# A fused routing-attention and SwiGLU kernel: a new start, later weight loads, and the norm ahead of the output products

## The chip, the cores and the metric

The kernel runs on one core of one Trainium2 chip. The metric is the device time of one execution in microseconds, lower is better. The reported time is the median of three runs. One more execution was taken by the hardware profiler, and all rows below come from that one.

## What is computed

Attention in which each query sees only the keys that were assigned to the same one of 16 centroids, then a gated feed-forward layer with an RMS norm. All inputs are float32. The shapes are q, k, v (4, 8, 768, 64), centroids (8, 16, 64), 3072 tokens of width 512 and a hidden width of 1536.

```python
q_assign = argmax(q_n @ c_n.T);  k_assign = argmax(k_n @ c_n.T)     # per head, 16 clusters
scores = where(q_assign[:, None] == k_assign[None, :], q @ k.T / 8, -1e9)
x = softmax(scores) @ v                                              # then heads side by side: (3072, 512)
xn = x / sqrt(mean(x * x) + 1e-6) * rms_g
out = (silu(xn @ w_gate) * (xn @ w_val)) @ w_out
```

## The kernel before

**Groups and units.** The 32 (batch, head) pairs form eight groups of four heads (`HG`). A group is prepared once: TensorE transposes q and k of each head (`trans`, L171, two parts of three 128x128 tiles), ScalarE copies the result out (L172), GpSimd and VectorE cast it to bfloat16 into `qext` and `kext` (L174, L175), GpSimd casts v (`vcast`, L178), and `scores_c` (L185) finds the cluster of each row: TensorE products with the centroids, four VectorE passes per half (L192, L196, L198, L203), and small DMAs that write one-hot rows under `qext` and `kext` (L206, L207). The score product then has 64 + 16 rows, so the mask comes out of the same product.

The attention itself runs in eight units u (`NU`), one for each half (384 queries) of a batch. A unit goes over eight heads h with three steps i each: `scores(u, h, i)` is two TensorE products into one of two PSUM tiles and one ScalarE exponential (L222). At i = 0, `pv` of the head before (L236) follows, and after each second head VectorE divides by the sum (L240, L242). Unit u uses groups 2b and 2b + 1 of its batch b = u // 2.

**Fill.** Between the steps, the main loop (L392 to L424) spreads a list of other work by a cost in front of each entry. In unit u these are the output products of unit u - 2 (`out_mm`, L318, nine pieces), the feed-forward of unit u - 1 (`rms`, `xtrans`, `gv`) and the preparation of group u + 2. `rms(u)` is three ScalarE squares over the last two heads (L254), a chain of eleven short VectorE operations on 128x3 numbers, and three scalings into `xn` (L279). TensorE can transpose `xn` (L288) only after that. The instruction order on every engine is the order of the code.

**Loads.** q and k have six staging buffers (`NQ`), v eight (`NV`). SP issues nearly all loads. The weights are cast in flight, on GpSimd's queue (`load_gv`, `load_o`). Before the first unit group 0 and half of group 1 are prepared; weights and the first loads of the second batch (`more`, L378) follow during it. The DMAs of SP and ScalarE share eight landing semaphores of the program, so an issue can wait for the landing of an earlier one.

Of the kernel before, what the change touches and what calls it, by code (L numbers as in the profile page):

```python
# [22 lines left out]
def kernel(  # L23
# [69 lines left out]
        load_qk(n, nc.scalar)  # L93
    for n in range(HG, NQ):
        load_qk(n)
    for n in range(HG):
        load_v(n, nc.scalar)
    gcol = const.tile([P, CC], F32)


# [2 lines left out]
    warm_ps = ps_s.tile([P, 2, 512], F32, tag="s", name="warm")  # L103
    for i in range(WARM):
        nc.tensor.matmul(warm_ps[:, i % 2], lhsT=warm[:, :P], rhs=warm, start=True, stop=True)


    ones = const.tile([P, P], F32)
# [18 lines left out]
        nc.gpsimd.memset(vbf[i][:, :, :, D:D + 1], 1.0)  # L127
    off = const.tile([P, 1], F32)
    nc.gpsimd.memset(off, -scale * ZS)


    c_sq = const.tile([P, D], F32)
    c_ss = const.tile([P, 1], F32)
    nc.vector.tensor_mul(c_sq, c_in, c_in)
    nc.vector.reduce_sum(c_ss, c_sq, axis=AX)
    c_inv = const.tile([P, 1], F32)
    nc.vector.reciprocal(c_inv, c_ss)
    nc.scalar.activation(c_inv, c_inv, ACT.Sqrt)
# [5 lines left out]
    c_ps = ps_g.tile([P, P], F32, tag="gen")
    nc.tensor.transpose(c_ps, c_n, ident_f)
    nc.vector.tensor_copy(cblk[:D, :, :NC], c_ps[:D].rearrange("d (h c) -> d h c", c=NC))
    nc.vector.tensor_copy(cblk[D:, :, NC:], c_ps[D:].rearrange("d (h c) -> d h c", c=NC))
# [13 lines left out]

    qkT = {}

    def trans(g, h, part):
        if (h, part) == (0, 0):
            qkT[g] = qk32.tile([P, HG, S], F32, tag="qkT", name="qkT")
        qk = staged[g * HG + h]
        ps = ps_g.tile([P, UQ], F32, tag="gen", name="tq")
        for i in range(HT):
            t = part * HT + i  # L170
            nc.tensor.transpose(ps[:, i * P:(i + 1) * P], qk[:, t].rearrange("p a d -> p (a d)"), ident_f)  # L171
        nc.scalar.copy(qkT[g][:, h, part * UQ:(part + 1) * UQ], ps)  # L172
        if part:
            nc.gpsimd.tensor_copy(qext[g % 4][:D, h], qkT[g][:D, h])  # L174
            nc.vector.tensor_scalar_mul(kext[g % 4][:D, h], qkT[g][D:, h], 1.0 / ZS)  # L175

    def vcast(n):
        nc.gpsimd.tensor_copy(vbf[n // HG % 4][:, n % HG, :, :D], stagedv[n])  # L178
# [3 lines left out]

    ohs = {}

    def scores_c(g, m, h0=0, h1=HG):  # L185
        ps = ps_g.tile([P, UQ], F32, tag="gen", name="sc")
        r = slice(32 * h0, 32 * h1)
        for h in range(h0, h1):
            nc.tensor.matmul(ps[32 * h:32 * h + 32], lhsT=cblk[:, g * HG % H + h],  # L189
                             rhs=qkT[g][:, h, m * UQ:(m + 1) * UQ], start=True, stop=True)  # L190
        sct = asg.tile([P, UQ], F32, tag="scT", name="scT", bufs=2)
        nc.vector.transpose(sct[r], ps[r])  # L192
        n = UQ // NC
        cl = sct[r].rearrange("p (n c) -> p n c", c=NC)
        mx = small.tile([P, n], F32, tag="mx", name="mx")
        nc.vector.tensor_reduce(mx[r], cl, axis=AX, op=ALU.max)  # L196
        ohT = asg.tile([P, UQ], BF16, tag="ohT", name="ohT", bufs=2)
        nc.vector.tensor_tensor(ohT[r].rearrange("p (n c) -> p n c", c=NC), cl,  # L198
                                mx[r].unsqueeze(2).broadcast_to([32 * (h1 - h0), n, NC]), op=ALU.is_equal)
        if m == 0:  # L200
            ohs[g, h0] = asg.tile([P, S], BF16, tag="oh", name="oh", bufs=2)
        oh = ohs[g, h0]
        nc.vector.transpose(oh[r, m * UQ:(m + 1) * UQ], ohT[r])  # L203
        if m:
            for h in range(h0, h1):
                nc.sync.dma_start(out=qext[g % 4][D:D + NC, h], in_=oh[32 * h:32 * h + NC])  # L206
                nc.sync.dma_start(out=kext[g % 4][D:D + NC, h], in_=oh[32 * h + NC:32 * h + 2 * NC])  # L207


    pT = {}  # L210
# [10 lines left out]
                             rhs=qext[g % 4][:KR, hh, hf * UQ:(hf + 1) * UQ], start=True, stop=True)  # L221
        nc.scalar.activation(pT[u, h][:, 2 * i:2 * i + 2], ps[:, :, :UQ], ACT.Exp, bias=off, scale=scale * ZS)  # L222

    xs, accs = {}, {}

    def pv(u, h):
        b = u // 2
        g, hh = b * 2 + h // HG, h % HG
        if h == 0:
            xs[u] = xp.tile([P, HT, DM], F32, tag="x", name="x", bufs=2)  # L230
        if h % 2 == 0:
            accs[u] = ps_a.tile([P, 2, HT, D + 1], F32, tag="acc", name="acc")
# [23 lines left out]
    def rms(u):  # L256
        x = xs[u]
        for t in range(HT):
            squares(u, t, True)
        ss = small.tile([P, HT], F32, tag="sm", name="sm")  # L260
        nc.vector.tensor_add(ss, sq[u][:, 0], sq[u][:, 1])
        ms = small.tile([P, HT], F32, tag="ms", name="ms")
        nc.vector.tensor_scalar(ms, ss, 1.0 / DM, 1e-6, op0=ALU.mult, op1=ALU.add)
        half = small.tile([P, HT], I32, tag="half", name="half")
        nc.vector.tensor_scalar(half, ms.bitcast(I32), 1, None, op0=ALU.logical_shift_right)
        yi = small.tile([P, HT], I32, tag="yi", name="yi")
        nc.vector.tensor_scalar(yi, half, -1.0, float(0x5F3759DF), op0=ALU.mult, op1=ALU.add)
        y = yi.bitcast(F32)
        for i in range(3):
            a = small.tile([P, HT], F32, tag="na", name="na")  # L270
            nc.vector.scalar_tensor_tensor(a, y, -0.5, y, op0=ALU.mult, op1=ALU.mult)
            a2 = small.tile([P, HT], F32, tag="nb", name="nb")
            nc.vector.tensor_mul(a2, a, ms)
            y2 = small.tile([P, HT], F32, tag="ny", name="ny")
            nc.vector.scalar_tensor_tensor(y2, a2, 1.5, y, op0=ALU.add, op1=ALU.mult)
            y = y2
        xn[u] = xp.tile([P, HT, DM], BF16, tag="xn", name="xn")
        for t in range(HT):
            nc.vector.tensor_scalar_mul(xn[u][:, t], x[:, t], y[:, t:t + 1])  # L279
# [48 lines left out]
            nc.sync.dma_start(out=rows[:, hf * HT + t], in_=o)  # L328


    def group_work(g, loads=True):
        w = []
        for h in range(HG):
            n = g * HG + h
# [1 line left out]

            def second(h=h, n=n):
                trans(g, h, 1)
                vcast(n)
                if loads:  # L340
                    load_qk(n + NQ)
                    load_v(n + NV)
            w.append((0.25, second))
# [14 lines left out]
        return w  # L358

    def ffn_work(u):  # L360
        w = [(0.0, lambda: rms(u))] + [(0.18, lambda c=c: xtrans(u, c)) for c in range(CC)]
        for f in range(FC):
            w.append((0.64, lambda f=f: gv(u, f, False)))
            w.append((0.64, lambda f=f: gv(u, f, True)))
        return w
# [2 lines left out]
        return [(0.86, lambda t=t, p=p: out_mm(u, t, p)) for t in range(HT) for p in range(3)]  # L368


    for h in range(HG):
        for part in range(2):
            trans(0, h, part)
        if NQ + h < H:
            load_qk(NQ + h)
        if h % 2:
            for m in range(2):
                scores_c(0, m, h - 1, h + 1)  # L378
    for n in range(HG, H):
        load_v(n)  # L380
    for h in range(HG):
        vcast(h)
        if h % 2:
            load_gv(h - 1)
    nc.sync.dma_start(out=gcol, in_=moe_rms_g.rearrange("(c p) -> p c", p=P), allow_slow_non_contiguous=True)
    first = group_work(1, False)
    for _, f in first[:4]:
        f()
    load_gv(1)
    load_gv(3)  # L390

    for u in range(NU):  # L392
        fill = []
        if u >= 2:
            fill += out_work(u - 2)
        prep = group_work(u + 2) if u + 2 < NG else []
        if u == 0:
            def more():
                for c in range(0, FC, 4):
                    load_o(c)  # L400
                for n in range(H, H + NV):
                    if n < H + NQ:
                        load_qk(n)
                    load_v(n)
            fill = first[4:] + [(0.0, more)] + prep
        elif u == 1:
            fill = prep[:4] + spread(ffn_work(0), prep[4:])
        else:
            fill += spread(ffn_work(u - 1), prep)
        total = sum(c for c, _ in fill)  # L410
# [47 lines left out]
```

## Time and profile before

| | |
|---|---|
| median of three runs | 449.36 us (447.55 to 450.74) |
| profiled execution | 448.44 us |
| its span in the profile | 446.7 us |
| TensorE busy, share of span | 370.0 us, 83% |
| ScalarE busy | 257.1 us, 58% |
| VectorE busy | 249.0 us, 56% |
| GpSimd busy | 57.9 us, 13% |
| mean granted TensorE clock | 0.907 |

The span is what the profile sees; 1.7 us of the execution's time lie around it. A matmul's end in the profile is modelled, so a busy TensorE may still be slow: the granted clock has to be read beside it (1.0 is 2.4 GHz, 0.5 is 1.2 GHz).

### The profile page before, as it was taken

How to read it: one execution, taken by the hardware profiler on the slowest of the kernel's cores; microseconds unless marked ns; L12 is line 12 of the kernel's file. 1: busy time of each engine (PE TensorE's matmuls, PEld its weight loads, DVE VectorE, ACT ScalarE, POOL GpSimd, SP SyncE). 2: the span in 40 equal slices, each digit the busy share in tenths (PEclk: the TensorE clock that was granted, in tenths of full speed). 3: DMA queues.
4: the chain of work that ended last, by engine and by line, in shares of the span. 5: the costliest groups of instructions: out<-in, count | busy, mean ns of one | idle time of the engine just before them, and what ended most of it. 6: DMA issues, size and time to landing. Idle time of an engine off the chain costs nothing.

```text
span 446.7 us, 7733 instructions
## 1 busy us (share of the span) xinstructions
PE 370.0 (83%) x3003; PEld 223.9 (50%) x3017; DVE 249.0 (56%) x550; ACT 257.1 (58%) x452; POOL 57.9 (13%) x84
## 2 busy tenths in 40 slices
PE   4793086699969998799969996999959995997896
PEld 1361063466536654566536653665536652663452
DVE  3764027567654784567557675478455535554441
ACT  1373088387836775377637873678536863783130
POOL 0627043111001210112002200121000000000000
PEclk8859589699988999899989999799979997999699
DMA  9598998422022422224113002000100010001001
GB/s 237 129 216 154 210 288 229 115 54 54 11 79 54 106 57 66 58 73 107 34 57 72 1 8 83 0 2 1 66 23 2 0 48 26 0 1 56 16 0 72
DMA packets 63732, 32.00 MB, mean 72 GB/s; under 512 B 52944, under 2 KB 59600, under 8 KB 63696
## 3 DMA queue, kind: packets, MB, share of 16 engines
q1 hardware_dynamic: 57248, 25.21, 20.9%
q0 software_dynamic: 2736, 4.72, 6.1%
q10 hardware_dynamic: 3712, 1.57, 1.3%
q8 instruction: 24, 0.39, 0.3%
q14 instruction: 12, 0.10, 0.1%
HBM read 28.35 MB, written 6.29 MB: 78 GB/s over the span
## 4 chain that ended last, share of the span: by engine, by line
PE 67%; DVE 13%; ACT 10%; DMA 6%; issue 3%; SPq 0%; ACTq 0%; DVEq 0%
PE o L323 14%; PE gate L299 13%; PE s L220 12%; PE val L299 12%; PE acc L236 7%; ACT pT L222 6%; PE tq L171 4%; PE sc L189 3%; DMA qk<-in_k_dram 2%; DVE xn L279 2%; DVE kext L175 2%; DMA qk<-in_q_dram 2%; PE tx L288 2%; ACT junk L254 2%; ACT qkT L172 1%
## 5 line engine op out<-in xcount | busy, mean ns | idle before, releaser
L222 ACT ACTIVATE pT<-s,off 128x768 bf16<-128x768 f32 x192 | 172.5, 902 | 87.2 <-PE s L220 86.8
L220 PE MATMUL s<-qext,kext 80*128 80x384 bf16 x384 | 99.9, 345 | 1.7 <-ACT pT L222 1.6
L299 PE MATMUL gate<-xnT,wg 128*128 128x384 bf16 x384 | 83.6, 342 | 0.8 <-DVE xnT L289 0.8
L299 PE MATMUL val<-xnT,wv 128*128 128x384 bf16 x384 | 80.2, 332 | 0.0
L309 DVE SCALAR_TENSOR_TENSOR gu<-th,gate 128x384 f32<-128x384 f32 x84 | 46.3, 551 | 52.1 <-ACT th L307 52.0
L323 PE MATMUL o<-wo,gvT 128*128 128x512 bf16 x274 | 68.2, 378 | 0.8
L174 POOL CAST qext<-qkT 64x768 bf16<-64x768 f32 x32 | 31.7, 991 | 241.5 <-ACT qkT L172 241.4
L171 PE MATMUL tq<-ident_f,qk 128*128 128x128 f32 x192 | 38.3, 326 | 21.8 <-DMA qk<-in_k_dram 17.3
L307 ACT ACTIVATE th<-gate 128x384 f32<-128x384 f32 x84 | 41.0, 488 | 26.7 <-PE gate L299 26.7
L220 PEld LDWEIGHTS <-kext 80*128 80x128 bf16 x384 | 38.0, 104 | 35.7 <-issue 12.2
L236 PEld LDWEIGHTS <-pT 128*128 128x128 bf16 x1152 | 47.9, 99 | 14.6 <-ACT pT L222 5.2
L236 PE MATMUL acc<-vbf,pT 128*128 128x65 bf16 x1152 | 51.5, 196 | 3.7 <-ACT pT L222 3.3
L314 DVE SCALAR_TENSOR_TENSOR gvT<-gu,val 128x384 bf16<-128x384 f32 x84 | 46.5, 554 | 11.8 <-PE val L299 5.1
L299 PEld LDWEIGHTS <-wg 128*128 128x128 bf16 x384 | 37.6, 102 | 25.5 <-issue 5.8
L299 PEld LDWEIGHTS <-wv 128*128 128x128 bf16 x384 | 37.2, 99 | 23.4 <-issue 1.9
L172 ACT COPY qkT<-tq 128x384 f32<-128x384 f32 x64 | 30.0, 478 | 32.1 <-issue 18.2
L175 DVE TENSOR_SCALAR kext<-qkT 64x768 bf16<-64x768 f32 x32 | 29.0, 912 | 34.3 <-ACT qkT L172 33.8
L288 PE MATMUL tx<-ident,xn 128*128 128x128 bf16 x96 | 15.4, 300 | 37.2 <-DVE xn L279 36.0
L171 PEld LDWEIGHTS tq<-ident_f,qk 128*128 128x128 f32 x192 | 28.3, 169 | 32.3 <-issue 19.1
L323 PEld LDWEIGHTS <-gvT 128*128 128x128 bf16 x288 | 26.7, 97 | 27.0
L326 DVE COPY o_sb<-o 128x512 f32<-128x512 f32 x24 | 16.6, 692 | 37.5 <-PE o L323 37.2
L288 PEld LDWEIGHTS <-xn 128*128 128x128 bf16 x96 | 9.9, 133 | 44.5 <-DVE xn L279 43.5
(56 smaller groups left out, 206.8 us busy)
## 6 DMA issues: line engine op xcount, KB each, us to landing
qk<-in_q_dram SPq DMA_DIRECT2D x32, 192.0 KB, 3.4
out_dram<-o_sb SPq DMA_DIRECT2D x24, 256.0 KB, 2.0
qk<-in_k_dram SPq DMA_DIRECT2D x28, 192.0 KB, 3.7
vs<-in_v_dram SPq DMA_DIRECT2D x28, 192.0 KB, 3.5
wg<-in_moe_w_gate_dram POOLq DMA_DIRECT2D x4, 384.0 KB, 5.8
wv<-in_moe_w_val_dram POOLq DMA_DIRECT2D x4, 384.0 KB, 7.2
wo<-in_moe_w_out_dram POOLq DMA_DIRECT2D x3, 512.0 KB, 11.6
qk<-in_k_dram ACTq DMA_DIRECT2D x4, 192.0 KB, 4.5
```

Source lines behind the costliest of these rows:

```text
L171: nc.tensor.transpose(ps[:, i * P:(i + 1) * P], qk[:, t].rearrange("p a d -> p (a d)"), ident_f)
L172: nc.scalar.copy(qkT[g][:, h, part * UQ:(part + 1) * UQ], ps)
L175: nc.vector.tensor_scalar_mul(kext[g % 4][:D, h], qkT[g][D:, h], 1.0 / ZS)
L220: nc.tensor.matmul(ps[:, j, :UQ], lhsT=kext[g % 4][:KR, hh, kc * P:(kc + 1) * P], rhs=qext[g % 4][:KR, hh, hf * UQ:(hf + 1) * UQ], start=T ...
L222: nc.scalar.activation(pT[u, h][:, 2 * i:2 * i + 2], ps[:, :, :UQ], ACT.Exp, bias=off, scale=scale * ZS)
L236: nc.tensor.matmul(acc[:, h % 2, t], lhsT=pT[u, h][:, kc, t * P:(t + 1) * P], rhs=vbf[g % 4][:, hh, kc], start=kc == 0, stop=kc == ST - 1)
L288: nc.tensor.transpose(ps[:, t * P:(t + 1) * P], xn[u][:, t, c * P:(c + 1) * P], ident)
L299: nc.tensor.matmul(ps, lhsT=w[:, c, f * P:(f + 1) * P], rhs=xnT[u][:, c], start=c == 0, stop=c == CC - 1)
L307: nc.scalar.activation(th, ps, ACT.Tanh, scale=0.5)
L309: nc.vector.scalar_tensor_tensor(gu, th, 1.0, ps, op0=ALU.add, op1=ALU.mult)
L314: nc.vector.scalar_tensor_tensor(gvT[u][:, f], gates[u], 0.5, ps, op0=ALU.mult, op1=ALU.mult)
L323: nc.tensor.matmul(outs[u], lhsT=gvT[u][:, f, t * P:(t + 1) * P], rhs=wo[:, f], start=f == 0, stop=f == FC - 1)
```

## The change

**Start.** The centroid norm is computed by a Newton iteration on VectorE in place of ScalarE's square root; ScalarE loads its exponential table at the very beginning. For group 0, ScalarE also writes `kext` from PSUM (new L194), the cluster scores take the PSUM tiles of the score product, and the one-hot DMAs are issued by ScalarE in place of SP. Four v loads are no longer on ScalarE's queue.

**Loads.** All weight loads stand behind the eight v casts of the first batch. The second batch's loads stand behind a small DMA (`hold`) that reads the reciprocal of heads 4 and 5 of unit 0.

**Order.** Group 2 is prepared in unit 1 with group 3, no longer in unit 0. `rms(u - 1)` is issued in the second step of unit u, ahead of the output products' later parts.

```diff
...
-    for n in range(HG):
-        load_v(n, nc.scalar)
+    for n in range(2):
+        load_v(n)
...
+    first_exp = const.tile([P, 1], F32)
+    nc.scalar.activation(first_exp, off, ACT.Exp)
...
-    c_inv = const.tile([P, 1], F32)
-    nc.vector.reciprocal(c_inv, c_ss)
-    nc.scalar.activation(c_inv, c_inv, ACT.Sqrt)
+    c_inv = rsqrt(c_ss, 1)
...
-        nc.scalar.copy(qkT[g][:, h, part * UQ:(part + 1) * UQ], ps)
-        if part:
-            nc.gpsimd.tensor_copy(qext[g % 4][:D, h], qkT[g][:D, h])
-            nc.vector.tensor_scalar_mul(kext[g % 4][:D, h], qkT[g][D:, h], 1.0 / ZS)
+        c = slice(part * UQ, (part + 1) * UQ)
+        nc.scalar.copy(qkT[g][:, h, c], ps)
+        if early:
+            nc.scalar.activation(kext[g % 4][:D, h, c], ps[D:], ACT.Copy, scale=1.0 / ZS)
...
-                nc.sync.dma_start(out=qext[g % 4][D:D + NC, h], in_=oh[32 * h:32 * h + NC])
-                nc.sync.dma_start(out=kext[g % 4][D:D + NC, h], in_=oh[32 * h + NC:32 * h + 2 * NC])
+                q_ = nc.scalar if early else nc.sync
+                q_.dma_start(out=qext[g % 4][D:D + NC, h], in_=oh[32 * h:32 * h + NC])
+                q_.dma_start(out=kext[g % 4][D:D + NC, h], in_=oh[32 * h + NC:32 * h + 2 * NC])
...
-        w = [(0.0, lambda: rms(u))] + [(0.18, lambda c=c: xtrans(u, c)) for c in range(CC)]
+        w = [(0.18, lambda c=c: xtrans(u, c)) for c in range(CC)]
...
+    def second_batch():
+        nc.sync.dma_start(out=hold, in_=invs[0].rearrange("p a t -> p (a t)"))
+        for n in range(H, H + NV):
+            if n < H + NQ:
+                load_qk(n)
+            load_v(n)
...
-        prep = group_work(u + 2) if u + 2 < NG else []
+        prep = group_work(u + 2) if 2 <= u < NG - 2 else []
...
-            fill = first[4:] + [(0.0, more)] + prep
+            fill = first[4:] + [(0.0, weights)]
         elif u == 1:
-            fill = prep[:4] + spread(ffn_work(0), prep[4:])
+            prep = group_work(2) + group_work(3)
+            fill = prep[:6] + spread(ffn_work(0), prep[6:])
...
-        gaps, done, n = 3 * H, 0.0, 0
+        gaps, done, n = 3 * H if u else 6, 0.0, 0
...
+                    if (u, h) == (0, H - 2):
+                        second_batch()
+                if (h, i) == (0, 1) and u:
+                    rms(u - 1)
...
     pv(NU - 1, H - 1)
+    rms(NU - 1)
     for _, f in out_work(NU - 2) + ffn_work(NU - 1) + out_work(NU - 1):
```

ScalarE's order at the start of the program, before (`qkT<-tq` copies a transposed head out, `pT<-s,off` is an exponential):

```order
L82 DMA qk<-in_k_dram 128x6x64 x4
L88 DMA vs<-in_v_dram 128x384 x4
L138 ACT_TABLE_LOAD
L138 ACTIVATE c_inv<-c_inv 128x1
L172 COPY qkT<-tq 128x384 x12
L222 ACT_TABLE_LOAD
L222 ACTIVATE pT<-s,off 128x768
```

The same engine after, from the last part of head 2 of group 0 to the first exponential (`oh` are the one-hots that VectorE makes):

```order
L192 COPY qkT<-tq 128x384
L194 ACTIVATE kext_147<-tq 64x384
L239 DMA qext_143<-oh 16x768
L240 DMA kext_147<-oh 16x768
...
L192 COPY qkT<-tq 128x384
L194 ACTIVATE kext_147<-tq 64x384
...
L239 DMA qext_143<-oh 16x768
L240 DMA kext_147<-oh 16x768
...
L192 COPY qkT<-tq 128x384 x4
L255 ACTIVATE pT<-s,off 128x768
```

The issues of the one-hots now stand between ScalarE's copies, four behind head 2 and four behind head 3.

VectorE's order at the start of unit 2, before (`inv` and `x` close a pair of heads, `o_sb` is an output row block, `sm` begins the norm, `xnT` follows the transposes of `xn`):

```order
L240 RECIPROCAL inv<-acc 128x6
L242 TENSOR_TENSOR x<-acc,inv 128x2x3x64
L326 COPY o_sb<-o 128x512 x2
L240 RECIPROCAL inv<-acc 128x6
L242 TENSOR_TENSOR x<-acc,inv 128x2x3x64
L326 COPY o_sb<-o 128x512
L261 TENSOR_TENSOR sm<-ss 128x3
...
L279 TENSOR_SCALAR xn<-x,ny 128x512 x3
L289 TENSOR_SCALAR xnT<-tx,gcol 128x384 x4
```

And after, at the same place:

```order
L274 RECIPROCAL inv<-acc 128x6
L276 TENSOR_TENSOR x<-acc,inv 128x2x3x64
L295 TENSOR_TENSOR sm<-ss 128x3
...
L301 TENSOR_SCALAR xn<-x,ny 128x512 x3
L348 COPY o_sb<-o 128x512 x2
L274 RECIPROCAL inv<-acc 128x6
L276 TENSOR_TENSOR x<-acc,inv 128x2x3x64
L348 COPY o_sb<-o 128x512
L311 TENSOR_SCALAR xnT<-tx,gcol 128x384 x4
```

The norm now stands directly behind the division of heads 6 and 7, and the three output copies behind it.

## Rows read from the trace of the kernel before

**Rows 1.** Waits: engine, line, waited for: us total, times, longest.

```profile
PE tx L288 <- DVE xn L279: 36.0, 13, 5.5
```

**Rows 2.** Stretches: busy us (x instructions) by engine, granted clock, DMA share, GB/s.

```profile
66.00:76.00 10.00, 7.42 (x89) 4.38 (x90) 6.42 (x13) 8.62 (x18) 1.75 (x3) 1.00 0.99 256
84.00:117.00 33.00, 32.74 (x308) 20.71 (x306) 20.96 (x41) 26.34 (x43) 3.20 (x4) 0.96 0.24 61
```

**Rows 3.** Timeline from the start of unit 2: start, us, instruction [idle before].

```profile
118.76 0.56 DVE L242 TENSOR_TENSOR x<-acc,inv 128x384 f32<-128x384 f32 x1
...
119.55 0.90 ACT L222 ACTIVATE pT<-s,off 128x768 bf16<-128x768 f32 x1 [1.48 <-PE s L220]
...
121.74 0.74 PE L236 MATMUL acc<-vbf,pT 128*128 128x65 bf16 x18
...
127.81 0.30 ACT L254 ACTIVATE junk<-x 128x128 bf16<-128x128 f32 x1
...
129.10 0.16 DVE L261 TENSOR_TENSOR sm<-ss 128x3 f32<-128x3 f32 x1
...
131.67 1.28 DVE L279 TENSOR_SCALAR xn<-x,ny 128x512 bf16<-128x512 f32 x3
...
132.22 1.40 PE L288 MATMUL tx<-ident,xn 128*128 128x128 bf16 x6 [3.87 <-DVE xn L279]
```

**Rows 4.** Timeline of TensorE: restarts in unit 1, unit 6 and behind unit 7.

```profile
82.17 2.07 PE L288 MATMUL tx<-ident,xn 128*128 128x128 bf16 x12 [5.51 <-DVE xn L279]
...
329.16 1.08 PE L288 MATMUL tx<-ident,xn 128*128 128x128 bf16 x3 [5.24 <-DVE xn L279]
...
415.06 1.19 PE L288 MATMUL tx<-ident,xn 128*128 128x128 bf16 x4 [3.75 <-DVE xn L279]
```

**Rows 5.** Seven stretches behind restarts (units 2 to 7, end): first, last, sum.

```profile
132.20:138.00 5.80, 5.38 (x25) 3.58 (x26) 2.51 (x7) 1.92 (x4) 0.00 (x0) 0.50 0.00 0
...
415.10:421.30 6.20, 5.98 (x26) 3.31 (x27) 2.65 (x7) 0.78 (x2) 0.00 (x0) 0.50 0.01 3
sum 40.00, PE 37.40 PEld 23.92 DVE 17.94 ACT 12.79 POOL 0.03; mean PE 5.34 PEld 3.42 DVE 2.56 ACT 1.83 POOL 0.00
```

**Rows 6.** Timeline: group 2's first transpose in unit 0, unit 1's first exponential.

```profile
55.87 0.87 PE L171 MATMUL tq<-ident_f,qk 128*128 128x128 f32 x3 [17.34 <-DMA qk<-in_k_dram]
...
74.46 0.89 ACT L222 ACTIVATE pT<-s,off 128x768 bf16<-128x768 f32 x1
```

**Rows 7.** Chain that ended last: start, us, what.

```profile
1.18 3.58 DMA qk<-in_q_dram
...
39.06 5.33 DMA qext<-oh
...
45.10 10.63 DMA qk<-in_k_dram
```

**Rows 8.** DMA queues, 48.6 to 48.7 us: packets, MB, share of 16 engines.

```profile
q0 software_dynamic: 16, 0.02, 96.2%
q1 hardware_dynamic: 11, 0.00, 21.3%
```

**Rows 9.** DMA queues over the whole span: GpSimd's queue, the weights.

```profile
q0 software_dynamic: 2736, 4.72, 6.1%
```

**Rows 10.** Timeline of the start.

```profile
11.28 0.48 ACT L172 COPY qkT<-tq 128x384 f32<-128x384 f32 x1 [1.66 <-PE tq L171]
...
14.66 0.57 DVE L192 STREAM_TRANSPOSE scT<-sc 64x384 f32<-64x384 f32 x1 [0.40 <-PE sc L189]
...
19.27 0.60 SPq L206 DMA_DIRECT2D qext<-oh  x1
...
27.19 0.90 ACT L222 ACTIVATE pT<-s,off 128x768 bf16<-128x768 f32 x1
```

**Rows 11.** Timeline of TensorE in unit 1: three transposes; eight cluster products.

```profile
97.57 0.49 PE L171 MATMUL tq<-ident_f,qk 128*128 128x128 f32 x3
...
109.86 0.85 PE L189 MATMUL sc<-qkT,cblk 128*32 128x384 f32 x8
```

More of the change, by code (lines that the diff above doesn't have):

```diff
@@ L105, with rsqrt @@
         nc.tensor.matmul(warm_ps[:, i % 2], lhsT=warm[:, :P], rhs=warm, start=True, stop=True)
+    def rsqrt(ms, n):
+        half = small.tile([P, n], I32, tag=f"half{n}", name="half")
+        nc.vector.tensor_scalar(half, ms.bitcast(I32), 1, None, op0=ALU.logical_shift_right)
+        yi = small.tile([P, n], I32, tag=f"yi{n}", name="yi")
+        nc.vector.tensor_scalar(yi, half, -1.0, float(0x5F3759DF), op0=ALU.mult, op1=ALU.add)
+        y = yi.bitcast(F32)
+        for i in range(3):
+            a = small.tile([P, n], F32, tag=f"na{n}", name="na")
+            nc.vector.scalar_tensor_tensor(a, y, -0.5, y, op0=ALU.mult, op1=ALU.mult)
+            a2 = small.tile([P, n], F32, tag=f"nb{n}", name="nb")
+            nc.vector.tensor_mul(a2, a, ms)
+            y2 = small.tile([P, n], F32, tag=f"ny{n}", name="ny")
+            nc.vector.scalar_tensor_tensor(y2, a2, 1.5, y, op0=ALU.add, op1=ALU.mult)
+            y = y2
+        return y
     ones = const.tile([P, P], F32)
@@ L143, with centroids_t @@
     nc.vector.memset(cblk, 0.0)
[L144 to L147, printed above, removed]
+    def centroids_t():
+        c_ps = ps_g.tile([P, P], F32, tag="gen", name="c_ps")
+        nc.tensor.transpose(c_ps, c_n, ident_f)
+        nc.vector.tensor_copy(cblk[:D, :, :NC], c_ps[:D].rearrange("d (h c) -> d h c", c=NC))
+        nc.vector.tensor_copy(cblk[D:, :, NC:], c_ps[D:].rearrange("d (h c) -> d h c", c=NC))
     wg = const.tile([P, CC, DF], BF16)
@@ L162, with trans @@
     qkT = {}
-    def trans(g, h, part):
+    def trans(g, h, part, early=False):
         if (h, part) == (0, 0):
@@ L171, in trans, with qcast, kcast @@
             nc.tensor.transpose(ps[:, i * P:(i + 1) * P], qk[:, t].rearrange("p a d -> p (a d)"), ident_f)
-        nc.scalar.copy(qkT[g][:, h, part * UQ:(part + 1) * UQ], ps)
-        if part:
-            nc.gpsimd.tensor_copy(qext[g % 4][:D, h], qkT[g][:D, h])
-            nc.vector.tensor_scalar_mul(kext[g % 4][:D, h], qkT[g][D:, h], 1.0 / ZS)
+        c = slice(part * UQ, (part + 1) * UQ)
+        nc.scalar.copy(qkT[g][:, h, c], ps)
+        if early:
+            nc.scalar.activation(kext[g % 4][:D, h, c], ps[D:], ACT.Copy, scale=1.0 / ZS)
+    def qcast(g, h):
+        nc.gpsimd.tensor_copy(qext[g % 4][:D, h], qkT[g][:D, h])
+    def kcast(g, h):
+        nc.vector.tensor_scalar_mul(kext[g % 4][:D, h], qkT[g][D:, h], 1.0 / ZS)
     def vcast(n):
@@ L183, with scores_c @@
     ohs = {}
-    def scores_c(g, m, h0=0, h1=HG):
-        ps = ps_g.tile([P, UQ], F32, tag="gen", name="sc")
+    scps = {}
+    def scores_c(g, m, h0=0, h1=HG, early=False):
+        if not early:
+            ps = ps_g.tile([P, UQ], F32, tag="gen", name="sc")
+        else:
+            if m == 0:
+                scps[g, h0] = ps_s.tile([P, 2, 512], F32, tag="s", name="sc")
+            ps = scps[g, h0][:, m, :UQ]
         r = slice(32 * h0, 32 * h1)
@@ L222, in scores @@
         nc.scalar.activation(pT[u, h][:, 2 * i:2 * i + 2], ps[:, :, :UQ], ACT.Exp, bias=off, scale=scale * ZS)
-    xs, accs = {}, {}
+    xs, accs, invs = {}, {}, {}
     def pv(u, h):
@@ L239, in pv @@
             inv = small.tile([P, 2, HT], F32, tag="inv", name="inv")
+            invs[u] = inv
             nc.vector.reciprocal(inv, acc[:, :, :, D])
@@ L263, in rms @@
         nc.vector.tensor_scalar(ms, ss, 1.0 / DM, 1e-6, op0=ALU.mult, op1=ALU.add)
[L264 to L276, printed above, removed]
+        y = rsqrt(ms, HT)
         xn[u] = xp.tile([P, HT, DM], BF16, tag="xn", name="xn")
@@ L328, in out_mm, with group_work @@
             nc.sync.dma_start(out=rows[:, hf * HT + t], in_=o)
-    def group_work(g, loads=True):
+    def group_work(g):
         w = []
@@ L338, in second @@
                 trans(g, h, 1)
+                qcast(g, h)
+                kcast(g, h)
                 vcast(n)
-                if loads:
+                if g > 1:
                     load_qk(n + NQ)
@@ L368, in out_work, with t0, weights @@
         return [(0.86, lambda t=t, p=p: out_mm(u, t, p)) for t in range(HT) for p in range(3)]
-    for h in range(HG):
+    def t0(h):
         for part in range(2):
-            trans(0, h, part)
+            trans(0, h, part, True)
+        qcast(0, h)
         if NQ + h < H:
             load_qk(NQ + h)
[L376 to L379, printed above, removed]
-        load_v(n)
+    first = group_work(1)
+    t0(0)
+    centroids_t()
+    t0(1)
+    for n in range(2, H):
+        load_v(n)
+    nc.sync.dma_start(out=gcol, in_=moe_rms_g.rearrange("(c p) -> p c", p=P), allow_slow_non_contiguous=True)
+    t0(2)
+    for m in range(2):
+        scores_c(0, m, 0, 2, True)
+    t0(3)
+    for m in range(2):
+        scores_c(0, m, 2, 4, True)
     for h in range(HG):
         vcast(h)
[L383 to L386, printed above, removed]
     for _, f in first[:4]:
         f()
-    load_gv(1)
-    load_gv(3)
+    def weights():
+        for c in range(CC):
+            load_gv(c)
+        for c in range(0, FC, 4):
+            load_o(c)
+    hold = const.tile([P, 2 * HT], F32)
+    def second_batch():
[4 more added lines that the diff above has]
+            load_v(n)
     for u in range(NU):
```

7 lines of the change are left out of this document (removed).

## The prediction

> **What bounds the kernel now.** I read the table of waits first. Its largest entry for TensorE is the transposes of the normed rows, which wait 36.0 us in 13 places for VectorE's `xn` [rows 1]. The stretches say why that matters: away from unit boundaries TensorE works 32.74 of 33 us, while ScalarE has 26.34 and VectorE 20.96 [rows 2]. So a microsecond that TensorE idles there is a microsecond of the end time. The timeline of unit 2's start shows how the wait comes about. `x` of heads 6 and 7 is done at 119.3, but the three squares begin only at 127.81, since they stand in ScalarE's queue behind seven exponentials, and VectorE's chain behind three output copies; `xn` begins at 131.67 and TensorE, which ran out of output products, idles 3.87 us [rows 3]. The same idle time is 5.24 us in units 6 and 7 (one row shown), 3.87 or 3.86 in units 2 to 5, 3.75 behind unit 7, and 5.51 in unit 1 [rows 3, 4].
>
> Each of these waits is followed by a slow stretch. In the seven windows behind the waits of units 2 to 7 and of the end, TensorE is busy 37.40 us with a granted clock of 0.50, the lower level of 1.2 GHz, or just above where the window reaches past it [rows 5]. Work that takes 37.4 us at half clock takes 18.7 us at full clock.
>
> The other large hole is in unit 0: TensorE stands still for 17.34 us until the first k of the second batch has landed [rows 6]. In the chain of waits that load took 10.63 us, a one-hot DMA before it 5.33 [rows 7]; in a short stretch then, GpSimd's queue (weights) held 96.2% of the DMA engines' time and SP's and ScalarE's kind of queue 21.3% [rows 8].
>
> **The norm ahead of the output products.** Nothing is added; three squares, eleven short operations and three scalings change place in seven units. The new chain in unit 2: `x` done at 119.3; the second exponential runs 119.55 to 120.45; squares 127.81 to 129.10 took 1.3 us, so now to 121.8; from the norm's first operation to the end of `xn` it took 129.10 to 132.95, 3.9 us, so now to 125.7 [rows 3]. TensorE's output products last until 132.22 - 3.87 = 128.35. The chain is hidden with 2.6 us to spare, and units 3 to 7 have the same order. Behind unit 7 out_work(6) covers it: 9 x 4 products, some 7.5 us, against 1 + 1.3 + 3.9 us.
>
> Gain: 4 x 3.87 + 2 x 5.24 + 3.75 = 29.7 us of idle time and 18.7 us of half clock, 48.4 us. Two things come off. The squares delay the third exponential of a unit: it now ends at about 121.8 + 0.9 = 122.7, and `pv`, which began at 121.74 [rows 3], needs it after its first four products; about 0.75 us in each of six units, 4.5 us. And the passage from the transposes over `xnT` to the first gate product contains four VectorE copies, so at full clock it doesn't halve; I take 0.5 us a unit, 3.0 us (an estimate; 0 to 1.2, a third of the 3.5 us that it took). The delayed output copies cost nothing: they are done before the transposes need their PSUM buffers. Sum 48.4 - 7.5 = **40.9 us**. Bounds: 48.4 if neither costs anything, 30 if the idle times go but most of the slow clock stays (29.7).
>
> On the clock, the Trainium skill ("TensorE: Matmul & The Clock Gate", Part 1, What's actually happening) says that for modeling the ramp penalty is under 1% of a typical kernel span. By that page, as an estimate, the clock's share would be at most some 4.5 us in place of 18.7, and the time below 14 us longer. The rows of half clock contradict it here: this kernel pays the ramp again at each unit.
>
> **The start.** New on ScalarE: eight casts of `kext`, which I price like the copy at 0.48 us, and eight DMA issues at 0.60 [rows 10]. Gone from it: the square root, a second table load, and four v issues, which held it back early. The first q has landed at 4.76 [rows 7], so transposes start at about 5 and ScalarE is through heads 0 and 1 at 9.4. Cluster products: 9.9. Eight VectorE passes of 0.57: 14.5. ScalarE, in order, waits for that, issues four DMAs: 16.9, copies and casts head 3, whose first half lets VectorE begin at 17.9; eight passes: 22.5; four issues: 24.9; four copies of group 1: 26.8. The first exponential comes at 26.9, where it was at 27.19 [rows 10]. I count **0**, with 3 us to either side: what the loads and the norm give, ScalarE's waits at its own DMA issues take.
>
> The Trainium skill ("DMA: Bandwidth & Descriptors", Issuing engines are not separate DMA queues) says that issuing from another engine saves only the issue time. Here the issue costs ScalarE more than it saves SP, as the chain above has it; by the rule too, the start gains nothing.
>
> **Loads and group 2.** In unit 0 ScalarE sets the pace without group 2: three exponentials of 0.90 and a short wait, some 2.9 us a head. Head 0 with four copies ends at 31.5, head 1 at 34.5, head 3 at 40.3. Weights stand behind the last v cast of group 1, so they start at about 32.5; GpSimd's queue took 6.1% of 16 engines x 446.7 us, that is 27.2 us of all engines [rows 9], so they end near 60 or 61. The one-hots of group 1 are made by 36.5 and meet the weights: 5.33 us to landing as in the trace [rows 7], 42.4 for head 4's pair, a wait of 2 us. Heads 4 and 5 end at 48.2, their reciprocal at 49.5; SP then issues the second batch, the first k at 50.5. It lands 10.63 us later if it crawls beside the weights as before [rows 7], at 61; the second head's k two us later. Unit 1 begins near 56 and its first four transposes stop TensorE until 63. Then a score product, its exponential to 65, and 132.22 - 127.81 = 4.4 us from squares to transposes [rows 3]: the feed-forward of unit 0 starts at 70, against 82.17 [rows 4]. That is 12.0 us. But unit 1 has more to do behind that point: six more sets of transposes at 0.49 and two more cluster products at 0.78 (one row, 0.85 as busy time) [rows 11], 4.5 us on a full TensorE. Gain **7.5 us**. Bounds: if the loads are in time, unit 1 runs from 53.5 with the old 82.17 - 74.46 = 7.7 us to its transposes [rows 4, 6], 61.2, gain 21 - 4.5 = 16.5. If the loads land 8 us later than forecast, 0.
>
> **Sum.** The profiled execution took 448.4 us. 448.4 - 40.9 - 0 - 7.5 = **400.0 us**. The median of the three runs lies 0.9 us above that execution, which I leave in the range.
>
> **The rivals.**
> 1. *The loads are in time.* The weights' queue leaves more than in the 0.1 us sampled, or the first unit runs slower than the loads. For: without weights beside it DMA moved 256 GB/s [rows 2]; against: the 10.63 us. 16.5 in place of 7.5: 391 us.
> 2. *The load wait moves whole.* TensorE loses in unit 1 what it lost in unit 0, with the norm of unit 0 behind it. Gain 0 or a little below, 408 to 411 us.
> 3. *The norm's wait shrinks, the slow clock stays.* If some short wait in each unit (for `xnT`, for the third exponential) is enough to keep the clock down, only the 29.7 us go, less 7.5: 448.4 - 22.2 - 7.5 = 419 us. Against: between 66 and 76 the clock stays at 1.00 with TensorE busy only 7.42 of 10 us [rows 2].
> 4. *Slower.* ScalarE takes its queue in order. If `x` of heads 6 and 7 comes late, the squares hold up the exponentials, and TensorE waits at the second step in every unit from 1 on. Now `x` is ready 1.1 us before the second exponential ends (119.3 against 120.45) [rows 3]. It costs all the delay beyond 1.1 us, once a unit. To outweigh 48.4 us it would have to be 7 us late in each of seven units; VectorE's load there speaks against it. Priced at 8 us: 448.4 + 56 - 48 = 456 us.
>
> **How the numbers follow.** Forecast case, 390 to 410 us: 0.60. Rival 1, near 391 and below: 0.13. Rival 2: 0.12. Rival 3: 0.10. Rival 4: 0.02. Both gains mostly lost for reasons that I don't see, within 1%: 0.03. A measurement here can tell about 1% from no change. The likeliest case gives 400. The range takes in rival 1 with all of the norm's 48.4 us, 448.4 - 16.5 - 48.4 = 383.5, and a start 1.5 us early, 382; at the other end rival 2 and most of rival 3, 417. Faster by over 1%: 0.94, within: 0.03, slower: 0.03.
>
> **What would show it.** Right: no wait of TensorE for `xn` above 1 us from unit 2 on, and one long stretch of clock 1.00 through units 2 to 7; the first exponential at 24 to 30 us; a wait for the second batch's k at the start of unit 1, not in unit 0; unit 1's transposes of `xn` at about 70. Wrong: a half clock inside units 2 to 7 without a long wait; a wait of ScalarE's squares for `x`; unit 1 starting its feed-forward after 78, which would undo the load part.

## The result and the profile after

The changed kernel took 404.94 us (median of four runs, 404.53 to 406.42) against 449.42 us for the kernel before. The ratio is 0.9019, its interval 0.8979 to 0.9060: 9.8% faster. The forecast was 400.0, so the time lies 4.9 us above it and inside the range. The profiled execution took 405.33 us with a span of 403.4 us; the mean granted clock is 0.941, TensorE is busy for 89% of the span, ScalarE 260.3 us.

TensorE's part of the table of waits, after:

```profile
PE tx L310 <- DVE o_sb L348: 5.5, 3, 2.0
PE sc L221 <- ACT qkT L192: 4.8, 1, 4.8
PE tx L310 <- DVE xn L301: 4.6, 1, 4.6
PE tq L190 <- DMA qk<-in_k_dram: 4.1, 3, 3.1
PE acc L269 <- ACT pT L255: 3.9, 10, 0.5
```

The 13 waits for `xn` [rows 1] have become one, the one of unit 1. The largest entry is new: transposes that wait for the copy of an output to SBUF, three times. The unit 2 stretch shows how the norm now passes:

```profile
117.19 0.56 DVE L276 TENSOR_TENSOR x<-acc,inv 128x384 f32<-128x384 f32 x1
...
117.45 0.90 ACT L255 ACTIVATE pT<-s,off 128x768 bf16<-128x768 f32 x1 [1.47 <-PE s L253]
...
118.25 0.30 ACT L288 ACTIVATE junk<-x 128x128 bf16<-128x128 f32 x1
...
119.53 0.16 DVE L295 TENSOR_TENSOR sm<-ss 128x3 f32<-128x3 f32 x1 [1.79 <-ACT junk L288]
...
120.35 0.62 PE L269 MATMUL acc<-vbf,pT 128*128 128x65 bf16 x14 [0.42 <-ACT pT L255]
...
122.11 1.28 DVE L301 TENSOR_SCALAR xn<-x,ny 128x512 bf16<-128x512 f32 x3
...
126.68 0.50 PE L310 MATMUL tx<-ident,xn 128*128 128x128 bf16 x6
```

The squares begin 1.06 us after `x` begins (9.05 us before, [rows 3]), `xn` is done at 123.39, and TensorE comes to its transposes only at 126.68, with no idle time ahead of them. All that the squares cost there is 0.42 us of `pv` at 120.35, where the third exponential comes late; it is 0.42 in each of units 2 to 7.

The stretch from 80.3 us to the end; the column PEclk is the granted clock:

```profile
core 0: us, PE busy (x) PEld busy (x) DVE busy (x) ACT busy (x) POOL busy (x), PEclk, DMA share, GB/s
80.30:404.50 324.20, 308.13 (x2676) 188.06 (x2688) 208.42 (x468) 218.25 (x386) 32.92 (x42) 1.00 0.19 53
```

The clock is 1.00 throughout; the seven slow stretches of before [rows 5] are gone, and TensorE is busy 95% of the time. Ahead of 80.3 us it is not. In unit 0 TensorE waits for the one-hots of group 1, and behind that wait it works at half clock up to unit 1:

```profile
45.11 0.82 PE L253 MATMUL s<-qext,kext 80*128 80x384 bf16 x2 [3.40 <-DMA kext<-oh]
...
48.59 0.80 PE L253 MATMUL s<-qext,kext 80*128 80x384 bf16 x2 [0.40 <-issue]
...
52.06 0.80 PE L253 MATMUL s<-qext,kext 80*128 80x384 bf16 x2 [0.40 <-issue]
```

```profile
45.00:61.00 16.00, 14.07 (x116) 8.33 (x116) 1.51 (x4) 12.19 (x19) 0.31 (x1) 0.50 1.16 206
```

A head takes 52.06 - 48.59 = 3.47 us there, and TensorE, busy for 14.07 of 16 us, sets the pace.

What is left stands in the timeline: unit 1's start, and the new wait, once with the copy that it waits for.

```profile
64.33 1.51 PE L190 MATMUL tq<-ident_f,qk 128*128 128x128 f32 x6 [3.14 <-DMA qk<-in_k_dram]
66.65 1.51 PE L190 MATMUL tq<-ident_f,qk 128*128 128x128 f32 x6 [0.80 <-DMA qk<-in_k_dram]
...
74.95 1.29 PE L310 MATMUL tx<-ident,xn 128*128 128x128 bf16 x5 [4.61 <-DVE xn L301]
...
213.60 0.69 DVE L348 COPY o_sb<-o 128x512 f32<-128x512 f32 x1 [1.72 <-DMA out_dram<-o_sb]
...
214.34 0.33 PE L310 MATMUL tx<-ident,xn 128*128 128x128 bf16 x3 [1.77 <-DVE o_sb L348]
```

The 17.34 us at 55.87 [rows 6] have become 3.14 and 0.80 us in unit 1. The first transposes of `xn` come at 74.95, where they came at 82.17 [rows 4]. At 213.60 VectorE copies the third output of a unit and waits 1.72 us for the first one's store to leave its buffer (there are two buffers); the transposes need the PSUM buffer that this copy frees. It happens in units 4 and 5 and behind unit 7 (1.77, 1.75, 2.00).

The start, on ScalarE, TensorE and VectorE:

```profile
15.80 0.62 ACTq L239 DMA_DIRECT2D qext<-oh  x1
...
18.39 0.48 ACT L192 COPY qkT<-tq 128x384 f32<-128x384 f32 x1 [6.23 <-issue]
...
18.92 1.49 PE L221 MATMUL sc<-qkT,cblk 128*32 128x384 f32 x2 [4.83 <-ACT qkT L192]
...
20.45 0.59 DVE L224 STREAM_TRANSPOSE scT<-sc 64x384 f32<-64x384 f32 x1 [4.67 <-PE sc L221]
...
27.98 1.24 ACT L192 COPY qkT<-tq 128x384 f32<-128x384 f32 x3 [7.58 <-DMA kext<-oh]
...
30.09 0.90 ACT L255 ACTIVATE pT<-s,off 128x768 bf16<-128x768 f32 x1 [0.16 <-PE s L253]
```

ScalarE stands before four issues at 15.80 to 18.35 and four at 25.44 to 27.88, does no work for 6.23 and 7.58 us, and TensorE waits for it 4.83 us. The first exponential comes at 30.09, 2.9 us later than before [rows 10].

### The profile page after: what moved, and what is told of

It is laid out like the page before. It is cut to its first block, busy times and chain, and to the rows that moved or that the text cites. A ratio compares the mean times of both kernels' runs of the same rounds, so it can differ in the third digit from the quotient of the medians.

```text
span 403.4 us, 7758 instructions
## 1 busy us (share of the span) xinstructions
PE 359.1 (89%) x3003; PEld 217.5 (54%) x3017; DVE 241.7 (60%) x556; ACT 260.3 (65%) x459; POOL 57.5 (14%) x84
## 4 chain that ended last, share of the span: by engine, by line
PE 69%; DVE 9%; ACT 9%; DMA 7%; issue 3%; ACTq 1%; SPq 1%; DVEq 0%
PE gate L321 15%; PE val L321 14%; PE s L253 13%; PE o L345 9%; PE acc L269 8%; PE tq L190 5%; ACT pT L255 4%; ACT junk L288 3%; DMA out_dram<-o_sb 3%; PE sc L221 3%; DMA qk<-in_q_dram 2%; DMA qk<-in_k_dram 2%; DVE o_sb L348 1%; DMA kext<-oh 1%; PE tx L310 1%
## 5 line engine op out<-in xcount | busy, mean ns | idle before, releaser
L253 PE MATMUL s<-qext,kext 80*128 80x384 bf16 x384 | 98.8, 343 | 5.6 <-DMA kext<-oh 3.4
L321 PE MATMUL gate<-xnT,wg 128*128 128x384 bf16 x384 | 79.6, 327 | 1.1 <-ACT qkT L192 1.0
L321 PE MATMUL val<-xnT,wv 128*128 128x384 bf16 x384 | 78.1, 325 | 0.2 <-DVE gvT L336 0.2
L269 PEld LDWEIGHTS <-pT 128*128 128x128 bf16 x1152 | 48.7, 101 | 15.6 <-ACT pT L255 5.8
L321 PEld LDWEIGHTS <-wg 128*128 128x128 bf16 x384 | 36.2, 98 | 24.1 <-issue 3.2
L190 PE MATMUL tq<-ident_f,qk 128*128 128x128 f32 x192 | 35.4, 311 | 10.3 <-DMA qk<-in_k_dram 4.1
L190 PEld LDWEIGHTS tq<-ident_f,qk 128*128 128x128 f32 x192 | 26.8, 161 | 20.3 <-ACT qkT L192 5.2
L200 DVE TENSOR_SCALAR kext<-qkT 64x768 bf16<-64x768 f32 x28 | 21.2, 758 | 15.8 <-ACT qkT L192 14.9
L274 DVE RECIPROCAL inv<-acc 128x6 f32<-128x6 f32 x32 | 6.0, 187 | 29.2 <-PE acc L269 29.1
L221 PE MATMUL sc<-qkT,cblk 128*32 128x384 f32 x128 | 17.5, 514 | 6.2 <-ACT qkT L192 4.8
```

The costliest lines, as they stand in the source:

```text
L253: nc.tensor.matmul(ps[:, j, :UQ], lhsT=kext[g % 4][:KR, hh, kc * P:(kc + 1) * P], rhs=qext[g % 4][:KR, hh, hf * UQ:(hf + 1) * UQ], start=T ...
L321: nc.tensor.matmul(ps, lhsT=w[:, c, f * P:(f + 1) * P], rhs=xnT[u][:, c], start=c == 0, stop=c == CC - 1)
```

## The experiments

Each was timed in three rounds beside the kernel before. Its ratio is to the kernel before in the same rounds (medians of 448.96 to 449.54 us). Differences are taken from 449.42 us (before) or 404.94 us (after).

**1. The norm's move alone, in the kernel before.**

```diff
-        w = [(0.0, lambda: rms(u))] + [(0.18, lambda c=c: xtrans(u, c)) for c in range(CC)]
+        w = [(0.18, lambda c=c: xtrans(u, c)) for c in range(CC)]
...
+                if (h, i) == (0, 1) and u:
+                    rms(u - 1)
...
+    rms(NU - 1)
```

> The kernel before with the norm's move alone: rms(u - 1) in the second step of unit u, and ahead of the last output products. Theory (the norm's move is the gain: 29.7 us of idle time and most of 18.7 us of half clock): 41 us less than before, 408 us, between 404 and 414; the 17 us load wait of unit 0 stays, and the clock is 1.00 from unit 2 to the end. Rival (start and loads carry the result): above 430 us.

Measured 409.11 us (407.18 to 411.97), ratio 0.9115 (0.9069 to 0.9160). The move alone gives 40.3 us. The load stall of unit 0 stays (16.4 us). In its profile the waits for an output copy appear too, 6.2 us in all, and behind the longest the clock falls; timeline and stretches:

```profile
379.26 0.80 PE L288 MATMUL tx<-ident,xn 128*128 128x128 bf16 x6 [3.51 <-DVE o_sb L326]
```

```profile
136.00:378.00 242.00, 236.03 (x2106) 145.16 (x2105) 162.98 (x370) 174.99 (x310) 25.31 (x32) 1.00 0.16 46
379.20:386.00 6.80, 6.74 (x28) 3.63 (x28) 2.43 (x7) 1.04 (x3) 0.00 (x0) 0.56 0.10 39
```

**2. The changed kernel without the norm's move** (the edit of 1 undone in it).

> The changed kernel with the norm put back as the first entry of the feed-forward list, so behind the output products. Theory: the idle times of 3.8 to 5.2 us and the half clock behind them return in units 2 to 7 and at the end, 40 us: 445 us, between 440 and 449, within 2% of before. Rival (start and loads carry the result): below 425 us.

Measured 447.54 us (445.58 to 448.07), ratio 0.9961 (0.9934 to 0.9988). Everything else in the change is worth 1.9 us here, which a measurement can hardly tell from none. The waits for `xn` are back in its table of waits, and so is the slow clock behind them (0.55 from 131.3 to 137 us):

```profile
PE tx L310 <- DVE xn L301: 35.2, 11, 5.2
```

Against the changed kernel the move is worth 42.6 us here, against 40.3 in experiment 1. So start and loads give 1.9 us without the move and 4.2 us with it. The intervals of these times are about 2 us to either side; the 3.51 us wait and the half clock behind it in experiment 1, which the changed kernel hasn't (its wait there is 2.00 us, at a clock of 1.00), are about as large as that difference. That they are its cause is argued, not shown.

**3. The wait kept, but filled.** In the kernel before, 16 products of ones that nothing reads run in each wait for `xn`.

```diff
+    def busy():
+        ps = ps_g.tile([P, 512], F32, tag="gen", name="busy")
+        for i in range(16):
+            nc.tensor.matmul(ps, lhsT=warm[:, :P], rhs=warm, start=True, stop=True)
...
-        w = [(0.0, lambda: rms(u))] + [(0.18, lambda c=c: xtrans(u, c)) for c in range(CC)]
+        w = [(0.0, lambda: rms(u)), (0.0, busy)] + [(0.18, lambda c=c: xtrans(u, c)) for c in range(CC)]
```

> The kernel before with 16 products of 512 columns of ones between the last output product and the transposes of xn, in all eight places; their result is not read. They fill the wait for xn with 3.45 us of TensorE work at full clock. Theory (idle time and slow clock are two separate costs): the wait itself stays, the half clock behind it goes, 15 to 18 us less: 432 us, between 428 and 438. Rival (behind the wait other engines set the pace, so the clock costs nothing): 447 to 452 us. Second rival (the products run past the end of the wait): above 452 us.

Measured 435.54 us (435.38 to 435.90), ratio 0.9699 (0.9680 to 0.9718): 13.9 us for nothing but busy work. Timeline of unit 2, and the stretch:

```profile
127.33 3.62 PE L363 MATMUL busy<-warm 128*128 128x512 bf16 x16
131.36 0.23 PE L288 MATMUL tx<-ident,xn 128*128 128x128 bf16 x1 [0.41 <-DVE xn L279]
```

```profile
62.00:321.00 259.00, 246.83 (x2154) 148.66 (x2152) 160.26 (x368) 178.35 (x316) 37.38 (x46) 1.00 0.24 66
```

`xn` comes no earlier in the unit (the transposes start 10.48 us after the start of `pv` in both kernels), yet the clock is 1.00 for 259 us and the units are shorter (46.74 us from unit 2's transposes to unit 3's, 48.95 before). So the slow clock was a cost of its own beside the idle time. The forecast's 18.7 us isn't fully recovered: in units 6 and 7 a wait of 1.79 us is left, and half clock behind it.

**4. The first group's one-hots issued by SP** in the changed kernel.

```diff
-                q_ = nc.scalar if early else nc.sync
+                q_ = nc.sync
```

> The changed kernel with the first group's one-hot DMAs issued by SP, as before, in place of ScalarE. Theory (ScalarE's own DMA issues, which wait for VectorE ahead of its copies, cost the start what it won): ScalarE copies head 3 right behind head 2 and VectorE's second pair begins at 15.8 us; SP is free at 21.9, so the first exponential moves from 30.1 to about 25.5 us and all behind it by some 4 us: 401 us, between 398 and 403. Rival (the start is not on the path, since unit 1 waits for the second batch anyway): first exponential earlier, but 404 to 406 us.

Measured 399.43 us (398.20 to 400.47), ratio 0.8885 (0.8836 to 0.8933): 5.5 us better than the changed kernel. ScalarE in its timeline:

```profile
19.49 1.95 ACT L192 COPY qkT<-tq 128x384 f32<-128x384 f32 x4 [4.48 <-PE tq L190]
23.48 0.90 ACT L255 ACTIVATE pT<-s,off 128x768 bf16<-128x768 f32 x1 [2.03 <-PE s L253]
```

The first exponential comes 6.6 us earlier, and unit 1's transposes of `xn` 6.7 us earlier (68.21). The start is on the path to the end nearly one for one, and it was ScalarE's own issues that held it.

**5. Three output buffers** in the changed kernel. Two scratch tiles are made smaller and two others share memory to make room for the third; the order of the instructions stays.

```diff
-    outp = pool("outp", 2)
+    outp = pool("outp", 3)
```

> The changed kernel with three buffers for output rows in place of two (room made by smaller scratch tiles). Theory (the 1.77 us in units 4 and 5 and the 2.0 us at the end, where TensorE waits for the third output copy, come from that copy's wait for the first output DMA): these three waits go, 5.5 us less than the changed kernel: 399.5 us, between 398 and 402. Rival (the copy would be late anyway, since it stands behind the norm on VectorE): 404 to 406 us.

Measured 400.20 us (399.49 to 401.08), ratio 0.8912 (0.8890 to 0.8934): 4.7 us better. The waits for the output copy are gone (0.45 us is left at the end). Where the transposes waited 1.77 us in unit 4, they now follow the output products without a wait:

```profile
210.88 1.02 PE L345 MATMUL o<-wo,gvT 128*128 128x512 bf16 x4
211.74 0.50 PE L310 MATMUL tx<-ident,xn 128*128 128x128 bf16 x6
```

**6. The second batch let go two heads earlier** in the changed kernel, while the weights still load.

```diff
-                    if (u, h) == (0, H - 2):
+                    if (u, h) == (0, 4):
```

> The changed kernel with the second batch's loads released two heads earlier, behind the reciprocal of heads 2 and 3. Theory (unit 1 waits 3.14 and 0.80 us for k since the loads are issued only at 54.7 us): issued near 47 us, the first two heads' loads land before unit 1 needs them, both waits go: 401 us, between 400 and 403. Rival (SP's loads crawl beside the weights until these are done at 63 us, whenever they are issued): 404 to 406 us, the waits stay.

Measured 406.54 us (404.92 to 409.59), ratio 0.9060 (0.9004 to 0.9116): nothing gained, as the rival had it. The issues come 6.7 us earlier, but the first k, issued at 48.69, took 16.2 us to land, and its wait is no shorter:

```profile
64.99 1.51 PE L190 MATMUL tq<-ident_f,qk 128*128 128x128 f32 x6 [3.57 <-DMA qk<-in_k_dram]
```

The DMA queues of that kernel between 55 and 61 us show what it met; q0 is GpSimd's (weights), q1 SP's and ScalarE's:

```profile
q0 software_dynamic: 933, 0.92, 90.6%
q1 hardware_dynamic: 932, 0.23, 29.7%
```

The two queues move the same number of packets, 933 and 932, but a packet of the weights carries 1 KB here and one of q, k and v 0.25 KB. So SP's loads get a fifth of the bytes in this stretch. The Trainium skill ("DMA: Bandwidth & Descriptors", Queues, rings and completion order) says that each DMA engine takes the queues with work in turn, a packet at a time; the equal counts in these rows fit that, though no run shows whether a packet of that rule is one of the profile's.

**7. Edits 4, 5 and 6 together.**

> Three output buffers, the first group's one-hots issued by SP and the second batch released behind the reciprocal of heads 2 and 3, together. Theory (three separate waits): 4.7 us as measured for the buffers, 4 for the one-hots, 4 for the second batch, less what overlaps: 393 us, between 390 and 397. Rival (only the buffers count): 399 to 401 us.

Measured 394.51 us (394.34 to 394.59), ratio 0.8784 (0.8747 to 0.8820). Edits 4 and 5 alone would give 404.94 - 5.5 - 4.7 = 394.7: they add, and edit 6 gives nothing here either (waits for k of 3.16 and 0.67 us stay).

**8. Gate and value weights issued earlier** in the changed kernel, right behind the first four v casts; the output weights stay where they were.

```diff
-    for _, f in first[:4]:
-        f()
-
     def weights():
         for c in range(CC):
             load_gv(c)
+
+    def weights_o():
         for c in range(0, FC, 4):
             load_o(c)
 
+    weights()
+    for _, f in first[:4]:
+        f()
...
-            fill = first[4:] + [(0.0, weights)]
+            fill = first[4:] + [(0.0, weights_o)]
```

> The changed kernel with the gate and value weights issued right behind the first group's v casts, near 23 us, in place of 35 us; the output weights stay where they are. Theory (the weights' transfer is what the one-hots of group 1 and the second batch meet): the weights are done by about 52 us, the 3.40 us wait for one-hots shrinks to under 2, the waits for the second batch's k go, the one-hots of the second pair of heads land 1 to 3 us later: 401 us, between 398 and 404. Rival (holding them back is what keeps the start free; early weights delay the first batch): 405 to 410 us.

Measured 402.16 us (401.86 to 403.98), ratio 0.8963 (0.8921 to 0.9005): 2.8 us better, with an interval that overlaps that of the changed kernel (0.8979 to 0.9060), so the gain rests on the trace as well. The weights are through before the second batch is let go; the queues between 54 and 60 us, and the loads that were issued in it:

```profile
q1 hardware_dynamic: 2959, 0.87, 61.3%
...
qk<-in_k_dram SPq DMA_DIRECT2D x3, 192.0 KB, 4.1
```

The same issue times as in the changed kernel (the first k at 55.52 against 55.40), but the first k lands after 3.8 us instead of 8.8, and no wait for a k is left in the table; the first twelve transposes follow without one, and unit 1's transposes of `xn` come at 70.30 instead of 74.95:

```profile
61.12 2.65 PE L190 MATMUL tq<-ident_f,qk 128*128 128x128 f32 x12
```

Together with 6 this settles the load wait: it depends on when the weights end, not on when the batch is let go. The other half of the theory failed: the wait for the one-hots of group 1, expected under 2 us, is still 3.31 us.

**9. Edits 4, 5 and 8 together.**

> The changed kernel with three of the edits that shortened it: three output buffers (measured -4.7 us alone), the one-hots of the first group issued by SP (-5.5 alone), gate and value weights issued right behind the first v casts (-2.8 alone). Theory: the three lie at different places (waits for the output copies in three later units; ScalarE's own issues ahead of the first exponential; loads of the second batch), so they add: 404.9 - 4.7 - 5.5 - 2.8 = 392 us, 389 to 395; the first exponential at 23 to 24, no wait of TensorE for k of the second batch above 1 us, no gap of transposes behind an output copy above 0.6. Rival: the first unit's one-hots on SP and the earlier weights meet on the DMA engines, and the first one-hots land later; then the early weights give nothing beside the earlier start: 394 to 396 us, first exponential after 24.5.

Measured 391.31 us (389.87 to 393.00), ratio 0.8701 (0.8665 to 0.8738). It is the fastest version here: 13% under the kernel before, 3.4% under the changed one. The sum of the three (392) holds, though one sign came out as the rival had it: the first exponential comes at 26.24, not at 23 to 24. Group 0's one-hots land later, as it said (the median for `kext` is 6.2 us, in experiment 4 2.0), and TensorE waits for the first of them 3.27 us, where it was 2.06 us. That is less than half of the 2.76 us to experiment 4. Most of the rest can't come from the weights, which are issued from 20.42 on: the last cluster products of group 0 already begin at 18.41, not at 17.07. No k is waited for. Timeline, and the stretch behind unit 1:

```profile
25.39 0.82 PE L253 MATMUL s<-qext,kext 80*128 80x384 bf16 x2 [3.27 <-DMA kext<-oh]
...
26.24 0.90 ACT L255 ACTIVATE pT<-s,off 128x768 bf16<-128x768 f32 x1 [3.55 <-PE s L253]
...
67.65 1.40 PE L310 MATMUL tx<-ident,xn 128*128 128x128 bf16 x6 [4.99 <-DVE xn L301]
```

```profile
72.60:390.00 317.40, 308.92 (x2691) 188.04 (x2689) 208.85 (x469) 217.98 (x386) 33.25 (x42) 1.00 0.19 54
```

TensorE is busy 97% of that stretch at full clock; what is left to win lies ahead of it, the half clock of unit 0 included: from 42 to 58 us TensorE is busy 14.00 of 16 us at a granted clock of 0.50 here too.

## Why the prediction came out as it did

The sum was 48.4 us of gain; the profiled executions give 448.44 - 405.33 = 43.1. The three terms can be measured in the two traces. From unit 1's transposes of `xn` to the end of the span it was 446.7 - 82.17 = 364.5 us, and is 403.4 - 74.95 = 328.5; the prediction moved 4.5 us of preparation into that part, so the norm's move gave 36.0 + 4.5 = 40.5. The 4.5 is the prediction's estimate, and no run measures it alone; it also stands, with the other sign, in the loads' share below. Ahead of that point 82.17 - 74.95 = 7.2 us were won, 4.5 of them for work that only moved behind it: 2.7 net. The first exponential is 2.9 us later, so the loads gave 5.6. (In the prediction's loads, 82.17 - 70 is 12.2 and not 12.0; its term would have been 7.7.)

| term | forecast | measured |
|---|---|---|
| norm's move | 40.9 | 40.5 in the traces; 40.3 and 42.6 (experiments 1, 2) |
| start | 0, 3 to either side | -2.9 |
| loads and group 2 | 7.5, bounds 0 and 16.5 | 5.6 |
| sum | 48.4 | 43.1 |

**The norm's move** was right in mechanism and in size, but two parts of the size were off and cancelled. Forecast was a loss of 0.75 us of `pv` in six units for the third exponential, 4.5 us; it is 0.42, some 2.5 us. Forecast were 3.0 us for the passage from transposes to gate products; in unit 2 no wait of TensorE above 0.2 us is left there. In their place came 5.5 us that the prediction had excluded with the sentence that the delayed output copies cost nothing, since they are done before the transposes need their PSUM buffers. The step left out a resource: the copies were checked against the PSUM buffers ahead of them, not against the two SBUF buffers behind them, which come free only when a store has landed. With three buffers 4.7 us of it are gone (experiment 5). So 7.5 us were taken off and some 8 us came off, in good part for another reason: that the size came out so close is in part luck.

**The clock** as a cost of its own is shown by experiment 3: 13.9 us without `xn` coming earlier, where half of the 37.4 us of [rows 5] is 18.7. Rival 3, that short waits might keep the clock down, failed: with a wait of 0.42 us in each unit and three near 2 us it stays at 1.00. The rule of the Trainium skill ("TensorE: Matmul & The Clock Gate", Part 1, What's actually happening) that for modeling the ramp penalty is under 1% of a typical kernel span doesn't hold for the kernel before: experiment 3 alone is 3.0% of its time.

**The start** was forecast at 0 and came out at -2.9, just inside its 3 us. The working had VectorE's first eight passes done at 14.5, and it was 15.8, since the transposes waited twice for a q, about 1 us each, ahead of the first cluster products. Then it had the second run begin at 17.9; it began at 20.45: ScalarE left its issues at 18.35, and TensorE, idle for 4.83 us behind them, did the next cluster products at half clock (1.49 us for two, in the row at 18.92). The issues stood in the chain, and were late by what came before them; the half clock did not stand in it. That the issues on ScalarE are what sets this chain was rightly said, and was called a draw; experiment 4 shows what it cost, 5.5 us.

**The loads** came out near the forecast's picture: the wait at the start of unit 1 and not of unit 0, k landing late beside the weights. It was milder than priced (8.8 us for the first k in place of 10.63, waits of 4.1 us in place of some 7), but the transposes of `xn` came at 74.95, not at 70. Three things lay ahead of them that the working had shorter: the first exponential came at 30.09 and not at 26.9; the wait for group 1's one-hots was 3.40 us and not 2; and a head in unit 0 behind it took 3.47 us and not 2.9, with TensorE at a clock of 0.50. The prediction looked for half clock behind the waits for `xn` alone and left it out here. So the first k was issued at 55.40, not at 50.5. Rival 1 (no wait) is what experiment 8 produces by moving the weights, for 2.8 us and not the 9 that it was priced at. Rival 2 (the whole wait moves) is out: 17.34 us became 4.1. Rival 4 is out: in unit 2 `x` is done at 117.75, and the squares begin at 118.25, behind the exponential and not behind `x`, which had ended 0.5 us earlier.

**What would show it**: the signs on the norm and the clock came true; so did the place of the load wait. Missed were the first exponential, at 30.1 just beyond 24 to 30, and the transposes of unit 1.

## What to carry to other kernels

When a step is moved past others on its engine, follow the buffers of those others on both sides, the one that they free and the one that they fill: a store's landing is part of the loop. A wait on TensorE costs more than its length if the clock falls behind it, and the granted clock of the stretch behind each long wait shows by how much. A load that shares the DMA engines with another queue should be priced by packet sizes: here, letting it go earlier was worth nothing while the other queue's larger packets were still in turn. Small DMAs that are issued by an engine on the critical path hold up what stands behind them in its order, with the waits ahead of each issue: 5.5 us here.

## What was unexpected of the hardware

The store that held the third output copy took 4.4 us from issue to landing in units 4 and 5, and 2.1 us in unit 2, for the same 256 KB. The queues between 209 and 213.6 us, after:

```profile
q1 hardware_dynamic: 287, 0.52, 30.7%
q8 instruction: 1, 0.02, 2.6%
...
out_dram<-o_sb SPq DMA_DIRECT2D x2, 256.0 KB, 4.4
```

and between 124 and 126.8 us:

```profile
q1 hardware_dynamic: 288, 0.52, 49.7%
...
out_dram<-o_sb SPq DMA_DIRECT2D x2, 256.0 KB, 2.1
```

In the first of them one packet of the instruction queue took 2.6% of 16 engines over 4.6 us, that is 1.9 us of one engine; in the second there is none. But the size of that packet doesn't give the delay: beside the store of unit 5, 4.4 us as well, it took 0.9 us, and beside the first store behind unit 7, which landed after 2.5 us, 0.9 us too. So what delays the store is open.

The length of a wait alone doesn't tell whether the clock falls behind it: behind 2.00 us of idle time at 375.01 in the changed kernel it stayed at 1.00, and behind 1.79 us in experiment 3 it fell; the two stretches, after and experiment 3:

```profile
375.00:381.00 6.00, 5.99 (x38) 3.47 (x38) 2.92 (x7) 1.81 (x4) 0.00 (x0) 1.00 0.12 44
```

```profile
321.00:326.00 5.00, 5.00 (x43) 3.36 (x41) 2.30 (x6) 2.29 (x3) 0.00 (x0) 0.66 0.01 3
```
